# Two of twelve probability tiles turned by TensorE instead of by a transposing transfer

## The chip, the cores and the metric

The kernel runs on one core of one Trainium2 chip. Its engines work side by side, each through its own instruction stream in order: TensorE (PE in the profile, with PEld for the loading of weights), VectorE (DVE), ScalarE (ACT), GpSimd (POOL) and SyncE (SP), which here only issues DMA transfers. The metric is the device time of one execution in microseconds, as the median of several runs.

## The reference

Four images of 12288 queries with 128 channels attend to keys that are pooled out of a 384 x 32 map. Then the 128 best rows of each image go through a small MLP.

```python
kv_pool = kv.reshape(B, H//4, 4, W//4, 4, C).mean(axis=(2, 4))   # 4 x 4 pooling, 768 keys
k = v = kv_pool.reshape(B, -1, C) @ w_sr
s = (q @ k.transpose(0, 2, 1)) / sqrt(C)
a = exp(s - s.max(-1)); a /= a.sum(-1) + 1e-9
x = a @ v                                                        # (4, 12288, 128)
scores = x @ w_gate                                              # top 128 rows of each image
out[rows] = x[rows] + sigmoid(scores[rows]) * (relu(x[rows] @ w1) @ w2)
```

## The kernel before

**Blocks.** The queries are cut into 192 blocks of 256 (48 to each of four batches). A block has two halves of 128 queries (`QT = 2`), each against all 768 keys (`M = 768`, six key tiles of 128, `KT = 6`). So a block holds a 128 x 1536 score tile in PSUM: half 0 in columns 0 to 767, half 1 in 768 to 1535. Two such score buffers, `s_buf[0]` and `s_buf[1]`, alternate from block to block; each fills three PSUM banks of 512 columns.

**What happens to a block.** `S` computes its scores in four parts of three matmuls (high and low parts of q and k), in the order 3, 2, 1, 0: part 3 is columns 1024 to 1535, part 2 is 768 to 1023, part 1 is 512 to 767, part 0 is 0 to 511. `s_max` on DVE finds the row maxima of both halves. `exp` on ACT exponentiates in three pieces: part 1 is columns 768 to 1279, part 2 is columns 1280 to 1535 (the last two key tiles of half 1, `CUT = 1280`), and part 0 is columns 0 to 767. Parts 0 and 1 go to an SBUF tile `am`; part 2 is written back into the score bank. Each value is then split into an f16 high part (`to_high`, ACT) and a bf16 rest (`to_low`: DVE for the last 256 columns, POOL for the other 1280), both in the SBUF tile `hl`. `turn` (L371) transposes the high half and then the low half of `hl` into the tile `at` by one DMA transpose each, of twelve 128 x 128 tiles, issued on SP. `AV` multiplies the twelve tiles of each half by the values, in 18 matmuls for each half of the queries (36 in all), into the banks `o_two`. `sums`, `recip` and `finish` on DVE normalise the result, and each second block issues its output on SP.

**Order.** The main loop (L601 to L645) writes the order of every engine by hand: `InOrder` (L39) chains the instructions of TensorE, DVE, ACT and POOL in program order. Iteration i runs `s_max(i)`, `AV(i - 4)` in two halves, `S(i + 1)`, `exp(i, 1)`, `exp(i, 2)`, `to_high(i, 1)`, the normalising of block i - 4, `to_low(i, 1)`, `exp(i, 0)`, `to_high(i, 0)`, `turn(i, 0)`, `to_low(i, 0)` and `turn(i, 1)`. So `AV` runs four blocks behind (`LAG = 4`). The SP queue takes its transfers in the order of the program: loads of q, loads of kv, outputs and the two transposes of each block.

**Beside the blocks.** During the first three batches `next_keys` prepares the keys of the next batch, a step at a time at the marked points of the loop: kv loads of half a megabyte, pooling sums on POOL, projections on TensorE. In the last batch there is none of this. `topk` of a finished batch runs in small steps in the next one; its counts and projections borrow the score buffer of block i - 1.

**Names in the profile.** All engine instructions go through the helper at L51, so they are told by their tiles: `m<-s` is `s_max`; `am<-s,m` with 512 columns is `exp` part 1, with 768 columns part 0; `s<-s,m` is `exp` part 2; `hl<-s` is `to_high` of the last 256 columns and `hl<-am` that of the other 1280; `hl<-s,hl` is `to_low` on DVE and `hl<-am,hl` that on POOL; `at<-hl` is a DMA transpose; `o_two<-vx,at` is `AV`; `s<-kh,qh`, `s<-kl,qh` and `s<-kh,ql` are `S`.

Of the kernel before, what the change touches and what calls it, by code (L numbers as in the profile page):

```python
# [6 lines left out]
F32 = mybir.dt.float32  # L7
F32R = mybir.dt.float32r
F16 = mybir.dt.float16
BF16 = mybir.dt.bfloat16  # L10
# [3 lines left out]
AF = mybir.ActivationFunctionType  # L14
ALU = mybir.AluOpType
AX = mybir.AxisListType
HALF = 256
PSUM = bass.MemoryType.PSUM

P = 128  # L20
B, N, C = 4, 12288, 128
HK, WK, R = 384, 32, 4
M = (HK // R) * (WK // R)
# [11 lines left out]
CUT = 2 * M - HALF  # L35
# [29 lines left out]
def attention_topk_mlp(ctx, tc, a, outs, capacity):  # L65
    nc = tc.nc
    pe, dve, act, pool = (InOrder(tc, e) for e in (nc.tensor, nc.vector, nc.scalar, nc.gpsimd))
# [6 lines left out]
    qp = ctx.enter_context(tc.tile_pool(name="qp", bufs=2))  # L74
    qs = ctx.enter_context(tc.tile_pool(name="qs", bufs=3))
    wk = ctx.enter_context(tc.tile_pool(name="wk", bufs=3))
    hlp = ctx.enter_context(tc.tile_pool(name="hlp", bufs=4))
    at = ctx.enter_context(tc.tile_pool(name="at", bufs=5))
    ob = ctx.enter_context(tc.tile_pool(name="ob", bufs=3))
# [10 lines left out]
    ident, tri, jrow, wg = (cst[:, i * P:(i + 1) * P] for i in range(4))  # L90
# [7 lines left out]
    s_flat = [x.rearrange("p k q -> p (k q)") for x in s_buf]  # L98
# [3 lines left out]
    banks = [o_two[:, j] for j in range(QT)]  # L102
# [11 lines left out]
    def borrow(bank):  # L114
        room["prep"], room["select"], room["count"] = bank[:, 0:HALF], bank[:, 512:1024], bank[:, 1024:1025]
# [13 lines left out]
    def load_q(b, ch, lo=0, hi=CHUNK):  # L129
        if (b, ch) not in qraw:  # L130
            qraw[b, ch] = qp.tile([P, CHUNK], F32, name="q_raw")
        nc.sync.dma_start(out=qraw[b, ch][:, lo:hi], in_=a["q"][:, b, ch, lo:hi])
# [123 lines left out]
    def next_keys(b):  # L256
        new_keys(b)
        raws = {}
        pend = []
        ready = None  # L260

        def after(kc):
            if kc % 2:
                pair = kc // 2
                pend.extend([lambda: (split_k(b, 2 * pair, 2 * pair + 2, 0), split_k(b, 2 * pair, 2 * pair + 2, 1)),
                             lambda: v_max(b, pair)])

        for kc in range(KT):
            if kc == 0:
                raws[0] = load_kv(b, 0)  # L270
            if kc + 1 < KT:
                raws[kc + 1] = load_kv(b, kc + 1, -2)
            t = raws[kc]
            pooled = kvs.tile([P, P], F32, name="pooled")
            u = kvs.tile([P, P, TAPS // 2], F32, name="kv_sum")
            t = t.rearrange("p h k t -> p (h k) t")
            adds = [(u[:, 32 * h:32 * h + 32], t[:, 32 * h:32 * h + 32, 0:8], t[:, 32 * h:32 * h + 32, 8:16]) for h in range(4)]
            adds += [(u[:, :, 0:4], u[:, :, 0:4], u[:, :, 4:8]), (u[:, :, 0:2], u[:, :, 0:2], u[:, :, 2:4]),
                     (pooled, u[:, :, 0], u[:, :, 1])]
            for h, (o, x, y) in enumerate(adds):  # L280
                if ready and h == 1:
                    yield from key_tile(b, kc - 1, ready)
                    after(kc - 1)
                yield "d"
                pool.tensor_tensor(out=o, in0=x, in1=y, op=ALU.add)
                if h == 3 and kc + 1 < KT:
                    load_kv(b, kc + 1, -2, raws[kc + 1])
                if pend:
                    pend.pop(0)()
            ready = pooled  # L290
        yield "d"
        yield from key_tile(b, KT - 1, ready)
        after(KT - 1)
        while pend:
            yield "d"
            pend.pop(0)()
        v_peak(b)
        start(vals, v_split(b))
# [12 lines left out]
    st = {}  # L311
# [12 lines left out]
    blocks = [(b, blk) for b in range(B) for blk in range(NBLK)]  # L324

    def S(n, parts=(0, 1, 2, 3)):
        b, blk = blocks[n]
        kh, kl = kvset[b]["kh"], kvset[b]["kl"]
        qh, ql = qsplit[b, blk]
        assert b == 0 or kvset[b].get("split") == KT  # L330
        for part in parts:
            lo, hi, j, k0 = ((0, 512, 0, 0), (512, 768, 0, 512), (768, 1024, 1, 0), (1024, 1536, 1, 256))[part]
            q = slice(j * P, (j + 1) * P)
            k = slice(k0, k0 + hi - lo)
            for i, (w, x) in enumerate(((qh, kh), (qh, kl), (ql, kh))):
                pe.matmul(s_flat[n % 2][:, lo:hi], w[:, q], x[:, k], start=(i == 0), stop=(i == 2))

    def s_max(n):
        m = sm.tile([P, QT], F32, name="m")
        dve.tensor_reduce(out=m, in_=s_flat[n % 2].rearrange("p (j k) -> p j k", j=QT), axis=AX.X, op=ALU.max, negate=True)  # L340
        st[n] = {"m": m}

    def exp(n, part):
        lo, hi, j = ((0, M, 0), (M, CUT, 1), (CUT, 2 * M, 1))[part]
        if part == 1:
            st[n]["a"] = wk.tile([P, CUT], F32, name="am")
        s = s_flat[n % 2][:, lo:hi]
        r = act.activation(s if part == 2 else st[n]["a"][:, lo:hi], s, AF.Exp, bias=st[n]["m"][:, j:j + 1])
        if part == 0:
            tc.declare_no_dep(r.ins, st[n]["low"], reason="both only read, other banks")  # L350

    def split_a(n, part):
        lo, hi = ((0, CUT), (CUT, 2 * M))[part]
        if part:
            st[n]["hl"] = hlp.tile([P, 2, QT * M], U16, name="hl")
            st[n]["at"] = at.tile([P, 2, QT * KT, P], U16, name="at")
        hl = st[n]["hl"]
        return (s_flat[n % 2][:, lo:hi] if part else st[n]["a"], hl[:, 0, lo:hi].bitcast(F16), hl[:, 1, lo:hi].bitcast(BF16))

    def to_high(n, part):  # L360
        a, ah, al = split_a(n, part)
        st[n][part] = a, ah, al
        act.copy(ah, a)

    def to_low(n, part, engine):
# [3 lines left out]
            st[n]["low"] = r.ins  # L369

    def turn(n, h):  # L371
        nc.sync.dma_start_transpose(out=st[n]["at"][:, h], in_=st[n]["hl"][:, h])

    def AV(n, j, dest=None):
        vx = kvset[blocks[n][0]]["vx"]
        assert kvset[blocks[n][0]].get("ready")
        ah, al = (st[n]["at"][:, h, j * KT:(j + 1) * KT].bitcast(t) for h, t in enumerate((F16, BF16)))
        if j == 0:
            st[n]["o"] = o_all if dest is None else dest
        o = st[n]["o"][:, j]  # L380
        mm = [(ah, h, kt) for kt in range(KT) for h in range(2)] + [(al, 0, kt) for kt in range(KT)]
        for i, (w, h, kt) in enumerate(mm):
            pe.matmul(o, w[:, kt], vx[:, h, kt], start=(i == 0), stop=(i == len(mm) - 1))
# [8 lines left out]
    def recip(n):  # L392
        dve.reciprocal(st[n]["rz"], st[n]["rz"])
# [182 lines left out]
    blocks = [(b, blk) for b in range(B) for blk in range(NBLK)]  # L576
# [7 lines left out]
    def start(tasks, gen):  # L584
        tasks.append([gen, next(gen)])
# [7 lines left out]
    def at_point(point):  # L593
        advance(vals, point)
        advance(prep, point)
        advance(select, point)

    start(vals, first_values())
    nb = len(blocks)
    LAG = 4  # L600
    for i in range(nb):  # L601
        old = i >= LAG
        b, blk = blocks[i]
        if blk % 2 == 0 and i + BPC < nb:
            nb_, nblk = blocks[i + BPC]
            load_q(nb_, nblk // BPC, nblk % BPC * BLK, (nblk % BPC + 2) * BLK)
        if blk == 0 and b + 1 < B:
            start(prep, next_keys(b + 1))
        if i:
            borrow(s_flat[(i - 1) % 2])  # L610
        s_max(i)
        if old:
            AV(i - LAG, 0)
            at_point("pe")
            AV(i - LAG, 1)
        else:
            at_point("pe")
            warm(18 if i == 0 else 36, banks[0][:, 0:P])
        if i % 2 == 0 and i + 2 < nb:
            split_q(*blocks[i + 2])  # L620
        at_point("ev")
        at_point("up")
        at_point("t")
        at_point("cmp")
        at_point("g")
        if 0 < i < nb - 1:
            S(i + 1, (3, 2, 1, 0))
        exp(i, 1)
        exp(i, 2)
        to_high(i, 1)  # L630
        if old:
            sums(i - LAG)
            recip(i - LAG)
            finish(i - LAG)
        to_low(i, 1, dve)
        exp(i, 0)
        to_high(i, 0)
        turn(i, 0)
        to_low(i, 0, pool)
        turn(i, 1)  # L640
        at_point("d")
        if i in (1, 2):
            advance(vals, "d")
        if old and blocks[i - LAG][1] == NBLK - 1:
            start(select, topk(blocks[i - LAG][0]))  # L645
    ended.append(True)
    room["select"], room["count"] = banks[1], banks[0][:, 0:1]
    n = nb - 1
# [23 lines left out]
    high, low, eqh, rest = (tk.tile([P, NCOL], U16, name=x) for x in ("high", "low", "eqh", "rest16"))  # L672
# [12 lines left out]
    for m in (n - 1, n):  # L685
        norm(m)
        lo = blocks[m][1] * QT
# [78 lines left out]
```

## Time and profile before

| what | us |
|---|---|
| median of 3 runs | 1013.18 |
| lowest and highest run | 1012.69 and 1016.16 |
| the profiled execution's own time | 1014.15 |
| its span, first to last instruction | 1012.3 |

The profiled execution ran with a mean granted TensorE clock of 0.967. In the lists of instructions, a row gives the start in us from the span's start, the duration in us, the engine, the line, the operation, output and inputs by tile, and the shapes; `xN` says that N such instructions in a row are merged; a bracket at the end gives the idle time of the engine before it and what ended it. Rows of waits give the engine that waited, what it waited for, the total in us, how often, and the longest. Rows by stretch give the stretch, its length and the busy time of each engine with the number of instructions in brackets; the last three numbers are the granted TensorE clock, the busy share of the DMA engines (over 1 where packets overlap) and GB/s.

### The profile page before, as it was taken

To read this page: it belongs to the slowest core of one execution; us is meant where nothing else is said; L and a number is where in the kernel's file an instruction comes from. 1 tells how busy PE (TensorE), PEld (TensorE's weight loads), DVE (VectorE), ACT (ScalarE), POOL (GpSimd) and SP (SyncE) were. 2 spreads that over 40 slices of the span, in tenths; PEclk is the share of its full clock that TensorE was granted. 3 is DMA by queue.
4 is the path that set the end of the run, shared out by engine and by line. 5 is a ranking of instruction groups with operands and counts; after the bars stand their busy time and mean duration, and the time that the engine had idled before them with its cause. 6 is when DMAs were issued, how large, how long until landed. Compare 5 with 4: busy or idle time off the path is not lost.

```text
span 1012.3 us, 25591 instructions
## 1 busy us (share of the span) xinstructions
PE 901.4 (89%) x9779; PEld 792.3 (78%) x9779; DVE 701.0 (69%) x1732; ACT 766.3 (76%) x1162; POOL 752.9 (74%) x573
## 2 busy tenths in 40 slices
PE   3889889898998989899899989999899999999954
PEld 2778777786887877787788878888788888888843
DVE  6557656564776777576767776787867887877675
ACT  2678768776898777687788876888888888889700
POOL 1579868777798878698679886898877777777700
PEclk9989989999999999899999999999999999999966
DMA  9799999999999999999999999999999999999920
GB/s 361 206 230 233 241 232 243 235 237 232 247 231 220 247 243 238 243 244 217 246 225 243 245 234 243 232 253 233 227 240 207 231 242 230 244 225 239 211 61 6
DMA packets 674235, 230.16 MB, mean 227 GB/s; under 512 B 606016, under 2 KB 656320, under 8 KB 673344
## 3 DMA queue, kind: packets, MB, share of 16 engines
q1 hardware_dynamic: 673856, 228.00, 110.5%
q8 instruction: 77, 1.26, 0.5%
q0 software_dynamic: 256, 0.52, 0.2%
q14 instruction: 46, 0.38, 0.1%
HBM read 52.04 MB, written 25.43 MB: 77 GB/s over the span
## 4 chain that ended last, share of the span: by engine, by line
PE 40%; DMA 19%; ACT 15%; DVE 12%; issue 7%; POOL 6%; SPq 0%; POOLq 0%; DVEq 0%; ACTq 0%
PE s L51 22%; PE o_two L51 18%; DMA at<-hl 17%; DVE m L51 7%; ACT am L51 7%; ACT hl L51 5%; POOL hl L51 3%; ACT s L51 2%; DMA kv_raw<-in_kv 2%; POOL ql L51 1%; POOL kv_sum L51 1%; DVE junk L51 1%; ACT qh L51 1%; DVE hl L51 1%; ACT kv_proj L51 0%
## 5 line engine op out<-in xcount | busy, mean ns | idle before, releaser
L51 POOL TENSOR_TENSOR hl<-am,hl 128x1280 bf16<-128x1280 f32 x192 | 505.6, 2633 | 168.2 <-ACT hl L51 88.2
L51 PEld LDWEIGHTS <-at 128*128 128x128 f16 (+1 forms) x6912 | 404.6, 98 | 120.0 <-DMA at<-hl 68.5
L51 PE MATMUL o_two<-vx,at 128*128 128x130 f16 x6804 | 444.8, 221 | 54.0 <-DMA at<-hl 47.8
L51 ACT ACTIVATE am<-s,m 128x512 f32<-128x512 f32 (+1 forms) x384 | 306.7, 799 | 124.9 <-DVE m L51 76.4
L51 DVE TENSOR_REDUCE m<-s 128x2 f32<-128x1536 f32 x192 | 337.2, 1756 | 85.2 <-PE s L51 84.7
L51 PE MATMUL s<-kh,qh 128*128 128x512 f32 (+1 forms) x768 | 278.9, 363 | 8.8 <-DVE rz L51 4.0
L51 PE MATMUL s<-kh,ql 128*128 128x512 f32 (+1 forms) x768 | 260.8, 340 | 1.6 <-POOL ql L51 1.5
L51 PE MATMUL s<-kl,qh 128*128 128x512 f32 (+1 forms) x768 | 260.6, 339 | 0.0
L51 ACT CAST hl<-am 128x1280 f16<-128x1280 f32 x192 | 241.7, 1259 | 6.1
L51 PEld LDWEIGHTS s<-kh,qh 128*128 128x128 f32 x768 | 146.6, 191 | 20.5 <-ACT s L51 5.0
L51 PEld LDWEIGHTS s<-kh,ql 128*128 128x128 f32 x768 | 145.8, 190 | 19.8 <-POOL ql L51 3.6
L51 PEld LDWEIGHTS s<-kl,qh 128*128 128x128 f32 x768 | 147.4, 192 | 9.0
L51 DVE TENSOR_TENSOR hl<-s,hl 128x256 bf16<-128x256 f32 x192 | 81.2, 423 | 76.5 <-ACT hl L51 69.2
L51 POOL TENSOR_TENSOR ql<-q_raw,qh 128x512 fp32r<-128x512 f32 x96 | 123.1, 1282 | 7.0 <-ACT qh L51 7.0
L51 ACT ACTIVATE s<-s,m 128x256 f32<-128x256 f32 x192 | 86.1, 448 | 6.3
L51 DVE TENSOR_TENSOR x<-o_two,rz 128x260 f32<-128x260 f32 x189 | 81.0, 429 | 6.4
L51 DVE TENSOR_SCALAR rz<-o_two,sg 128x2 f32<-128x2 f32 x189 | 41.0, 217 | 60.3 <-PE o_two L51 59.8
L51 ACT CAST hl<-s 128x256 f16<-128x256 f32 x192 | 71.5, 373 | 6.9 <-DMA at<-hl 0.7
L51 ACT CAST qh<-q_raw 128x512 fp32r<-128x512 f32 x96 | 58.9, 613 | 1.1 <-DMA q_raw<-in_q 1.1
L51 POOL TENSOR_TENSOR kv_sum<-kv_raw 128x256 f32<-128x256 f32 x72 | 52.6, 731 | 0.0
L51 PEld LDWEIGHTS <-ones 128*128 128x128 bf16 (+1 forms) x291 | 24.5, 109 | 17.2 <-issue 13.3
L51 DVE RECIPROCAL rz<-rz 128x2 f32<-128x2 f32 x192 | 31.9, 166 | 6.6
(157 smaller groups left out, 438.9 us busy)
## 6 DMA issues: line engine op xcount, KB each, us to landing
out<-x SPq DMA_DIRECT2D x96, 256.0 KB, 3.2
q_raw<-in_q SPq DMA_DIRECT2D x93, 256.0 KB, 3.9
kv_raw<-in_kv SPq DMA_DIRECT2D x36, 512.0 KB, 5.2
kv_raw<-in_kv SPq DMA_DIRECT2D x6, 1024.0 KB, 8.4
at<-hl SPq DMA_TRANSPOSE x384, 4.6
w<-in_w SPq DMA_DIRECT2D x2, 512.0 KB, 9.5
q_raw<-in_q SPq DMA_DIRECT2D x1, 768.0 KB, 8.2
cst<-in_cst SPq DMA_DIRECT2D x1, 320.0 KB, 9.7
```

What stands on the lines that cost most here:

```text
L51: r = f(*args, **kwargs)
```

## The change

In the blocks of the first three batches (144 of 192; `by_pe`), the last two key tiles of half 1 take another way. `exp` part 2 writes to a new SBUF tile `ae` instead of back into the score bank. TensorE transposes the two 128 x 128 f32 tiles of `ae` into the place in the score bank that they came from (`turn_pe`). `to_high` and `to_low` of these 256 columns then read the transposed values from the bank and write straight into `at`. The two DMA transposes of the block shrink from twelve tiles to ten. To make room in the order, `S(i + 1)` is cut in two: parts 3 and 2, then the transposes, then parts 1 and 0; `exp` part 0 moves ahead of `to_high(i, 1)` on ACT. The last batch keeps the old way, but for the allocation of its tiles.

```diff
+    wke = ctx.enter_context(tc.tile_pool(name="wke", bufs=2))
...
+    def by_pe(n):
+        return blocks[n][0] < B - 1
+
     def exp(n, part):
         lo, hi, j = ((0, M, 0), (M, CUT, 1), (CUT, 2 * M, 1))[part]
         if part == 1:
             st[n]["a"] = wk.tile([P, CUT], F32, name="am")
-        s = s_flat[n % 2][:, lo:hi]
-        r = act.activation(s if part == 2 else st[n]["a"][:, lo:hi], s, AF.Exp, bias=st[n]["m"][:, j:j + 1])
-        if part == 0:
-            tc.declare_no_dep(r.ins, st[n]["low"], reason="both only read, other banks")
-
-    def split_a(n, part):
-        lo, hi = ((0, CUT), (CUT, 2 * M))[part]
-        if part:
             st[n]["hl"] = hlp.tile([P, 2, QT * M], U16, name="hl")
             st[n]["at"] = at.tile([P, 2, QT * KT, P], U16, name="at")
-        hl = st[n]["hl"]
-        return (s_flat[n % 2][:, lo:hi] if part else st[n]["a"], hl[:, 0, lo:hi].bitcast(F16), hl[:, 1, lo:hi].bitcast(BF16))
+        s = s_flat[n % 2][:, lo:hi]
+        if part == 2:
+            out = s
+            if by_pe(n):
+                out = st[n]["ae"] = wke.tile([P, HALF], F32, name="ae")
+        else:
+            out = st[n]["a"][:, lo:hi]
+        r = act.activation(out, s, AF.Exp, bias=st[n]["m"][:, j:j + 1])
+        if part == 0:
+            st[n]["exp0"] = r.ins
+            if "low" in st[n]:
+                tc.declare_no_dep(r.ins, st[n]["low"], reason="both only read, other banks")
+
+    def turn_pe(n):
+        for c in range(2):
+            lo = CUT + c * P
+            r = pe.transpose(s_flat[n % 2][:, lo:lo + P], st[n]["ae"][:, c * P:(c + 1) * P], ident)
+            tc.declare_no_dep(r.ins, st[n]["exp0"], reason="other banks")
+
+    def halves(n, part):
+        lo, hi = ((0, CUT), (CUT, 2 * M))[part]
+        a = s_flat[n % 2][:, lo:hi] if part else st[n]["a"]
+        if part and by_pe(n):
+            hl = [st[n]["at"][:, h, CUT // P:].rearrange("p t q -> p (t q)") for h in range(2)]
+        else:
+            hl = [st[n]["hl"][:, h, lo:hi] for h in range(2)]
+        return a, hl[0].bitcast(F16), hl[1].bitcast(BF16)
...
     def turn(n, h):
-        nc.sync.dma_start_transpose(out=st[n]["at"][:, h], in_=st[n]["hl"][:, h])
+        k = CUT if by_pe(n) else 2 * M
+        nc.sync.dma_start_transpose(out=st[n]["at"][:, h, 0:k // P], in_=st[n]["hl"][:, h, 0:k])
...
-        if 0 < i < nb - 1:
-            S(i + 1, (3, 2, 1, 0))
+        more = 0 < i < nb - 1
+        if more:
+            S(i + 1, (3, 2))
         exp(i, 1)
         exp(i, 2)
+        if by_pe(i):
+            exp(i, 0)
+            turn_pe(i)
+        if more:
+            S(i + 1, (1, 0))
         to_high(i, 1)
         if old:
             sums(i - LAG)
             recip(i - LAG)
             finish(i - LAG)
         to_low(i, 1, dve)
-        exp(i, 0)
+        if not by_pe(i):
+            exp(i, 0)
         to_high(i, 0)
         turn(i, 0)
```

More of the change, by code (lines that the diff above doesn't have):

```diff
@@ L346, in exp @@
             st[n]["a"] = wk.tile([P, CUT], F32, name="am")
-        s = s_flat[n % 2][:, lo:hi]
-        r = act.activation(s if part == 2 else st[n]["a"][:, lo:hi], s, AF.Exp, bias=st[n]["m"][:, j:j + 1])
-        if part == 0:
-            tc.declare_no_dep(r.ins, st[n]["low"], reason="both only read, other banks")
-    def split_a(n, part):
-        lo, hi = ((0, CUT), (CUT, 2 * M))[part]
-        if part:
             st[n]["hl"] = hlp.tile([P, 2, QT * M], U16, name="hl")
             st[n]["at"] = at.tile([P, 2, QT * KT, P], U16, name="at")
-        hl = st[n]["hl"]
-        return (s_flat[n % 2][:, lo:hi] if part else st[n]["a"], hl[:, 0, lo:hi].bitcast(F16), hl[:, 1, lo:hi].bitcast(BF16))
+        s = s_flat[n % 2][:, lo:hi]
[23 more added lines that the diff above has]
+        return a, hl[0].bitcast(F16), hl[1].bitcast(BF16)
     def to_high(n, part):
-        a, ah, al = split_a(n, part)
-        st[n][part] = a, ah, al
+        st[n][part] = a, ah, al = halves(n, part)
         act.copy(ah, a)
```

## The prediction

> **What bounds the kernel now.** I read the page first, then the stretches between batches, the waits in each, and the SP queue in order of time.
>
> ```profile
> span 1012.3 us, 25591 instructions
> ...
> PE 901.4 (89%) x9779; PEld 792.3 (78%) x9779; DVE 701.0 (69%) x1732; ACT 766.3 (76%) x1162; POOL 752.9 (74%) x573
> ...
> at<-hl SPq DMA_TRANSPOSE x384, 4.6
> ```
>
> PE is busiest, but no engine is full. So I split the loop at the row maxima of blocks 1, 48, 96, 144 and 191. The rows show the work on tile hl; POOL does one subtraction to a block, so its count is the number of blocks.
>
> ```profile
> 35.00:273.20 238.20, 19.83 (x47) 76.21 (x94) 123.74 (x47) 0.96 1.17 234
> 273.20:512.50 239.30, 20.32 (x49) 78.32 (x96) 126.21 (x48) 0.99 1.17 236
> 512.50:743.00 230.50, 20.28 (x48) 78.34 (x97) 126.38 (x48) 0.99 1.19 237
> 743.00:953.00 210.00, 19.94 (x47) 76.63 (x94) 124.05 (x47) 1.00 1.17 231
> ```
>
> The first three batches take 708.0 us for 143 blocks, 4.95 us each; the last takes 4.47. The DMA share and the GB/s are the same in all four, though the pace is not: a sign that transfers set it. The chain of waits shows what a block costs PE where nothing is late:
>
> ```profile
> 425.13 1.05 PE o_two L51 x18
> 426.18 0.00 PE s L51
> 426.18 1.05 PE o_two L51 x18
> 427.23 2.18 PE s L51 x12
> 429.41 1.05 PE o_two L51 x18
> ```
>
> From 425.13 to 429.41, that is 4.28 us. Over 143 blocks it makes 612 us of the 708. The waits of the four stretches, one row from each in order, say what most of the remaining 96 us are:
>
> ```profile
> PEld L51 <- DMA at<-hl: 23.8, 22, 2.7
> ...
> PEld L51 <- DMA at<-hl: 27.8, 28, 2.9
> ...
> PEld L51 <- DMA at<-hl: 10.5, 12, 2.9
> ...
> PEld L51 <- DMA at<-hl: 4.7, 6, 1.6
> ```
>
> In the three batches PE waits 62.1 us for transposed tiles, in the last 4.7. The other 34 us are projections, counts, the MLP, a lower clock in batch 0 and short waits. Why the tiles are late is seen in the SP queue, here with the POOL subtraction of one block and two rows that sum up a longer stretch (the SP transposes begun in it, and the work on hl).
>
> ```profile
> 457.57 2.62 POOL L51 TENSOR_TENSOR hl<-am,hl 128x1280 bf16<-128x1280 f32 x1 [0.89 <-ACT hl L51]
> ...
> 464.35 6.35 SPq L372 DMA_TRANSPOSE at<-hl  x2
> 470.80 0.53 SPq L408 DMA_DIRECT2D out<-x  x1
> 471.38 0.49 SPq L132 DMA_DIRECT2D q_raw<-in_q  x1
> 471.98 7.20 SPq L372 DMA_TRANSPOSE at<-hl  x4
> 479.27 0.53 SPq L408 DMA_DIRECT2D out<-x  x1
> 479.90 1.27 SPq L124 DMA_DIRECT2D kv_raw<-in_kv  x1
> 481.27 4.65 SPq L372 DMA_TRANSPOSE at<-hl  x2
> ...
> L372 SPq DMA_TRANSPOSE at<-hl x32: 1410/1802/4413, 438.6 to 517.5; - x32
> ...
> 438.50:520.70 82.20, 6.77 (x16) 26.84 (x33) 43.18 (x17) 1.00 1.18 232
> ```
>
> Each SP row begins within 0.11 us of the end of the one before: SP is never free here. The block whose subtraction ended at 460.19 has its two transposes issued only from 464.35. The stretch of 16 blocks takes 82.2 us, 5.14 a block, at 232 GB/s: this is what the SP queue and its DMA rings can do while kv is loaded, and it is slower than PE's 4.28. So in the three batches the bound alternates: transfers while the queue is backlogged, PE when it has caught up.
>
> **The change part by part.**
>
> *Smaller transposes.* A transpose moves 128 x 1536 x 2 B = 393 KB; ten tiles instead of twelve take 65.5 KB off each, 131 KB off a block. Traffic in the three batches is (238.2 x 234 + 239.3 x 236 + 230.5 x 237) / 143 = 1167 KB a block; after, 1036 KB. The last batch, without kv, moves 210.0 x 231 / 47 = 1032 KB a block. So the three batches get the traffic that batch 3 has, where PE waited 4.7 us in 47 blocks, 0.1 each. Over 143 blocks that is 14 us, and the waits fall from 62 to 14: **-48 us**. The bounds: to nothing (-62) if PE's slower pace leaves the queue still more room, and unchanged (0) if a transpose costs SP and the rings its 1.8 us whatever its size. No row has a ten-tile transpose. I take the share by size, since a plain output of 256 KB holds SP 0.53 us and a transpose 1.8: issue follows what is issued, not its number. At 232 GB/s the backlogged stretch would need (82.2 x 232 / 16 - 131) / 232 = 4.58 us a block.
>
> *Two transposes on PE.* Two f32 transposes of another tile stand between AV matmuls in the trace.
>
> ```profile
> 728.38 0.20 PEld L51 LDWEIGHTS s<-cst,mx 128*128 128x128 f32 x2
> 728.44 0.38 PE L51 MATMUL s<-cst,mx 128*128 128x128 f32 x2
> 728.65 1.13 PE L51 MATMUL o_two<-vx,at 128*128 128x130 f16 x17
> ...
> L51 PE MATMUL s<-cst,xe x3: 276/276/278, 508.6 to 953.9; 128*128 128x128 f32 x3
> ```
>
> The stream moves on after 728.65 - 728.44 = 0.21 us for both, though one shows 276 ns from its start to its modelled end. They lie fully on PE's path: 144 x 0.21 = **+30 us**, to 144 x 2 x 0.276 = 79 us if they don't overlap their neighbours. The Trainium skill (TensorE: Matmul & The Clock Gate, "Part 4: PE-mode transpose") reports about 275 ns for a bf16 transpose in one kernel, most of it access latency. Its figure is the row's duration; as an occupancy it would give the 79 us, against the 0.21 that the row's successor shows.
>
> *PE waits for ACT.* This is new: the transposes stand behind S parts 3 and 2 and wait for exp part 2; behind them queue S parts 1 and 0, and behind those the next row maxima.
>
> ```profile
> 409.79 1.76 DVE L51 TENSOR_REDUCE m<-s 128x2 f32<-128x1536 f32 x1 [0.94 <-PE s L51]
> 411.64 0.69 ACT L51 ACTIVATE am<-s,m 128x512 f32<-128x512 f32 x1 [1.90 <-DVE up L51]
> 411.66 0.50 PE L51 MATMUL s<-kh,qh 128*128 128x512 f32 x1
> 412.36 0.45 ACT L51 ACTIVATE s<-s,m 128x256 f32<-128x256 f32 x1
> 412.82 0.28 PE L51 MATMUL s<-kh,qh 128*128 128x256 f32 x1
> 412.84 0.37 ACT L51 CAST hl<-s 128x256 f16<-128x256 f32 x1
> 413.11 0.91 ACT L51 ACTIVATE am<-s,m 128x768 f32<-128x768 f32 x1
> 413.30 0.42 DVE L51 TENSOR_TENSOR hl<-s,hl 128x256 bf16<-128x256 f32 x1 [0.29 <-ACT hl L51]
> 414.05 1.26 ACT L51 CAST hl<-am 128x1280 f16<-128x1280 f32 x1
> 414.06 1.76 DVE L51 TENSOR_REDUCE m<-s 128x2 f32<-128x1536 f32 x1 [0.34 <-PE s L51]
> ```
>
> Exp part 2 ends at 412.81, and PE comes to part 1 of S (the second PE row) at 412.82. With the 0.09 us from one engine to the next (the cast ends at 413.21, DVE starts at 413.30) PE would wait 0.08 us: 12 us over 144 blocks. It is less if exp part 2, which no longer writes the bank that part 1 reads, follows it as closely as exp part 0 follows the cast (0.10 before its end) instead of 0.03 after part 1's. Between 0 and 12 I take **+6 us**. Where PE itself was late, ACT is done long before.
>
> *ACT and DVE reordered.* ACT's work is the same; only exp part 0 goes ahead of the cast, so the cast and DVE's to_low start later, and the next row maxima stand behind to_low on DVE. The loop is exp 1, exp 2, exp 0, cast, to_low, maxima: starts 0.72 and 0.48 and 0.94 apart, then 0.37 + 0.09 + 0.42 + 1.76 + 0.09 = 4.87 us if every step waits for the one before. Steps without such a wait overlap by 0.10 instead of standing 0.03 apart, 0.13 less each, so exps and cast need 0.59 + 0.35 + 0.81, and the loop 4.48: equal to PE's 4.28 + 0.21 = 4.49. I cost it at nothing, covered by PE's own block, since exp 2, exp 0 and the cast then have different outputs and no step needs the one before it on ACT. If that cover is gone, it is the rival below.
>
> *The sum:* 30 + 6 - 48 = -12 us. The profiled execution took 1014.15 us (1.9 around its span), which makes 1002; it lies 1.0 above the median of the runs, so 1001 for the median.
>
> **The rivals.**
>
> *Nothing moves (1013).* The issue of a transpose has a fixed price, or kv bursts keep the queue full. Then transfers still set the pace, and PE's 36 us fall into its 62 us of waits. For it: issue times vary from 1.4 to 4.4 us at one size. Against it: batch 3, with 1032 KB, has nearly no waits.
>
> *The DVE loop closes (1032, slower).* If ACT's steps still wait for each other, the loop of 4.87 us exceeds PE's 4.49 by 0.38. Blocks that wait for a tile anyway (22 + 28 + 12 = 62 by the rows) don't pay; the other 81 do: 31 us, 1001 + 31. For it: exp 1 and exp 2 stand 0.03 apart today, which looks like a wait. Against it: that wait goes with the in-place write. It decides as soon as the next maxima start later than PE's scores allow.
>
> *Transposes cost their duration (1050).* The 79 us instead of 30 add 49. Against it: the successor's start.
>
> *The clock falls (1020).* If two transposes in each block lower PE's activity as the clock gate counts it, the granted clock of batches 1 and 2 goes to batch 0's 0.96 too and batch 0's falls as far: 143 x 4.49 = 642 us of PE work x 0.03 = 19 us, 1020. Against it: the 0.99 to 1.00 of batches 1 to 3, where PE pauses for tiles far longer than 0.2 us. The Trainium skill (TensorE: Matmul & The Clock Gate, "Part 4: PE-mode transpose") says that a transpose doesn't count as a busy PE; the few in this trace can't show it.
>
> *All waits vanish (983).* -62 + 30 + 0 = -32, less 1 to the median gives 981 to 983.
>
> **How the numbers follow.** The forecast has 0.48 (own range 990 to 1010), nothing moves 0.19, the DVE loop 0.14, all waits vanish 0.09, transposes at duration 0.05, clock 0.05. About 0.5% (5 us) is what a measurement of this kernel can tell from no change. Of the forecast 0.06 lies within it. Faster: 0.42 + 0.09 = 0.51, and a part of the "nothing moves" case, 0.03, makes 0.54. Same: 0.06 + 0.16 = 0.22. Slower: 0.24. The range, 983 to 1030, leaves out most of the loop case and all of the transposes at duration.
>
> **What would show it.** Right: the three batches take some 696 us, PE's wait for at<-hl falls below 20 us in them, the SP rows show gaps, and a quiet stretch steps at 4.49. Transposes at about 0.1 us each by their successors' starts. Wrong: SP rows still without gaps and median issue still 1.8 us (nothing moves); maxima that wait for DVE's to_low or ACT, and quiet steps near 4.87 (the loop); PE idle before the transposes for more than 0.1 us a block.

## The result and the profile after

The changed kernel took 989.06 us (median; 987.28 to 989.85) against 1014.67 for the kernel before: a ratio of 0.974, with a 95% interval of 0.971 to 0.977. In a later comparison the same code took 989.97 us, ratio 0.981 (0.977 to 0.985). So it is faster by some 2 to 2.6%, the two intervals spanning 1.5 to 2.9%; 1001 was forecast, with a range of 983 to 1030. The profiled execution took 988.30 us, 25.9 less than the one before.

The stretches between the row maxima of blocks 1, 48, 96, 144 and 191, as before (work on tile hl; the last three numbers are clock, DMA share and GB/s):

```profile
35.00:258.50 223.50, 0.00 (x0) 59.66 (x47) 123.64 (x47) 0.98 1.12 226
258.50:489.30 230.80, 0.00 (x0) 61.71 (x49) 126.26 (x48) 0.99 1.11 220
489.30:718.80 229.50, 0.00 (x0) 61.59 (x49) 126.25 (x48) 1.00 1.04 208
718.80:925.60 206.80, 19.96 (x47) 75.95 (x94) 124.09 (x47) 1.00 1.16 229
```

The three batches take 683.8 us instead of 708.0. Their traffic rate was 234 to 237 GB/s and is now below the 229 of batch 3: transfers no longer set the pace. The backlog of the SP queue went with it. In the kernel before, SP began the first transpose of a block 4.50, 4.93 and 2.37 us (the medians of the three batches) after POOL's subtraction for that block had ended; in the changed kernel it begins 0.15, 0.02 and 1.14 us before that end. The clock is no lower than before. The chain of waits over two quiet blocks:

```profile
414.68 2.39 PE s L51 x14
417.07 1.05 PE o_two L51 x18
418.12 1.05 PE o_two L51 x18
419.17 2.41 PE s L51 x14
421.58 1.05 PE o_two L51 x18
```

A step is 4.51 us from AV to AV (417.07 to 421.58) and 4.49 from S to S (414.68 to 419.17), against 4.28: take 4.50, 0.22 more, for the two transposes among the 14 PE instructions of S. The chain of work that ended last, from the page of the profile before and then after, is now PE's:

```profile
PE 40%; DMA 19%; ACT 15%; DVE 12%; issue 7%; POOL 6%; SPq 0%; POOLq 0%; DVEq 0%; ACTq 0%
...
PE 75%; DVE 10%; ACT 5%; DMA 2%; issue 1%; SPq 0%; POOLq 0%; ACTq 0%; DVEq 0%
```

Of PE's waits (the list over the three batches, and the groups of weight loads over the whole run):

```profile
PEld s L51 <- ACT ae L51: 12.8, 22, 3.5
...
L51 PEld LDWEIGHTS s<-cst,ae 128*128 128x128 f32 x288 | 31.3, 141 | 8.5 <-ACT ae L51 7.5
L51 PEld LDWEIGHTS s<-kh,qh 128*128 128x128 f32 x768 | 146.0, 190 | 18.8 <-ACT ae L51 5.3 <-DVE mg L51 3.9
```

The list over the three batches has no row any more in which PE or PEld waits for `at<-hl`; it was 62.1 us. Of the 12.8 us that are put down to ae, only the 7.5 before the transposes' own weight loads are the new wait. The 5.3 before S's first loads were there in the kernel before under another name:

```profile
L51 PEld LDWEIGHTS s<-kh,qh 128*128 128x128 f32 x768 | 146.6, 191 | 20.5 <-ACT s L51 5.0 <-DVE mg L51 3.2 <-ACT hs L51 1.4
```

Nearly half of the 7.5 us is one wait of 3.5 us, at 287.50. Ahead of it two DVE instructions of `topk` (`key`) took 1.12 and 2.60 us, where the kernel before shows 0.41 and 0.70 for them. The second, here with the POOL subtraction beside it, held up the row maxima, and with them ACT's exps:

```profile
281.89 2.63 POOL L51 TENSOR_TENSOR hl<-am,hl 128x1280 bf16<-128x1280 f32 x1
282.04 2.60 DVE L51 TENSOR_TENSOR key<-key,sc 128x96 int32<-128x96 int32 x1
...
286.39 0.69 ACT L51 ACTIVATE am<-s,m 128x512 f32<-128x512 f32 x1 [4.73 <-DVE m L51]
```

It ends 0.12 us after POOL's subtraction; in the kernel before it ran beside a POOL sum of 0.73 us and ended 0.11 us after that. So the new order put it next to a longer POOL instruction.

The transposes themselves, in the timeline, and ACT and DVE around them:

```profile
418.96 0.69 ACT L51 ACTIVATE am<-s,m 128x512 f32<-128x512 f32 x1 [1.23 <-DVE up L51]
419.55 0.47 ACT L51 ACTIVATE ae<-s,m 128x256 f32<-128x256 f32 x1
419.90 0.90 ACT L51 ACTIVATE am<-s,m 128x768 f32<-128x768 f32 x1
420.14 0.38 PE L51 MATMUL s<-cst,ae 128*128 128x128 f32 x2
420.28 0.36 PE L51 MATMUL s<-kh,qh 128*128 128x256 f32 x1
420.48 0.28 PE L51 MATMUL s<-kl,qh 128*128 128x256 f32 x1
420.60 0.28 PE L51 MATMUL s<-kh,ql 128*128 128x256 f32 x1
420.69 0.38 ACT L51 CAST at<-s 128x256 f16<-128x256 f32 x1
421.10 0.42 DVE L51 TENSOR_TENSOR at<-s,at 128x256 bf16<-128x256 f32 x1 [0.77 <-ACT at L51]
421.62 1.76 DVE L51 TENSOR_REDUCE m<-s 128x2 f32<-128x1536 f32 x1
```

S goes on 0.14 us after the first transpose starts, and its first matmul then holds PE 0.20 us, 0.08 more than the 0.12 of the next one: together 0.22. The exps stand 0.59 and 0.35 apart, as the forecast had them. The next maxima start 0.10 us after DVE's subtraction ends, so they wait for something else: by the semaphores in the trace, 113 of the 144 maxima of the three batches start within 0.04 us of the signal of S's last matmul. So PE's path sets the step, and DVE's loop has a little room.

The SP queue, batch 1 (transposes: least, median and greatest issue time in ns), before and then after:

```profile
L372 SPq DMA_TRANSPOSE at<-hl x96: 1285/1557/5115, 272.0 to 511.4; - x96
```

```profile
L393 SPq DMA_TRANSPOSE at<-hl x97: 1253/1356/5000, 257.3 to 488.0; - x97
```

The median fell to 0.87, near 10/12 = 0.83; the least time hardly moved. So what got shorter is chiefly the part of an issue above its least time. How much of that part is a wait for the queue and how much a wait for `hl` these rows don't tell.

### The profile page after: what moved, and what is told of

Its sections match the earlier page's. It is cut to its first block, busy times and chain, and to the rows that moved or that the text cites. A ratio compares the mean times of both kernels' runs of the same rounds, so it can differ in the third digit from the quotient of the medians.

```text
span 986.5 us, 26037 instructions
## 1 busy us (share of the span) xinstructions
PE 920.9 (93%) x10067; PEld 819.4 (83%) x10067; DVE 697.9 (71%) x1732; ACT 727.1 (74%) x1162; POOL 753.4 (76%) x573
## 3 DMA queue, kind: packets, MB, share of 16 engines
q8 instruction: 79, 1.29, 0.5%
## 4 chain that ended last, share of the span: by engine, by line
PE 75%; DVE 10%; ACT 5%; DMA 2%; issue 1%; SPq 0%; POOLq 0%; ACTq 0%; DVEq 0%
PE s L51 42%; PE o_two L51 33%; DVE m L51 5%; ACT am L51 3%; DMA at<-hl 2%; DVE junk L51 2%; ACT ae L51 1%; DVE at L51 0%; DVE key L51 0%; ACT hl L51 0%; ACT at L51 0%; ACT s L51 0%; ACT kv_proj L51 0%; DVE hit L51 0%; SPq L393 0%
## 5 line engine op out<-in xcount | busy, mean ns | idle before, releaser
L51 PEld LDWEIGHTS <-at 128*128 128x128 f16 (+1 forms) x6912 | 399.8, 97 | 62.7 <-issue 55.6
L51 PE MATMUL o_two<-vx,at 128*128 128x130 f16 x6804 | 433.2, 220 | 5.4 <-POOL vx L51 2.4
L51 PE MATMUL s<-kh,qh 128*128 128x512 f32 (+1 forms) x768 | 291.1, 379 | 7.5 <-DVE rz L51 4.1
L51 ACT CAST hl<-am 128x1280 f16<-128x1280 f32 x192 | 245.2, 1277 | 1.5
L51 DVE TENSOR_TENSOR at<-s,at 128x256 bf16<-128x256 f32 x144 | 61.1, 424 | 141.8 <-ACT at L51 135.6
L51 ACT CAST at<-s 128x256 f16<-128x256 f32 x144 | 54.6, 379 | 19.0 <-PE s L51 18.8
L51 ACT ACTIVATE ae<-s,m 128x256 f32<-128x256 f32 x144 | 67.4, 468 | 0.0
L51 PE MATMUL s<-cst,ae 128*128 128x128 f32 x288 | 57.5, 281 | 4.8 <-ACT ae L51 4.6
```

Of the source, the lines that this page charges most:

```text
L51: r = f(*args, **kwargs)
```

## The experiments

Theory A: the queue of transfers was the bound of the three batches, the smaller transposes relieve it, and TensorE pays 0.22 us a block. Rival B: the gain is ACT's shorter chain, since the exps now overlap and `hl` is ready earlier. Rival C: a transfer costs the same whatever its size. A last question was whether the loop over DVE, forecast as a rival, exists at all. In the expectations, the "13 us of waits for ae" is the 12.8 of the list; the split of it into 7.5 and 5.3 was made after.

### The relief undone

Twelve tiles go by transfer again; the tiles that TensorE turned stay in the tail of `hl` and are read there.

```diff
-        k = CUT if by_pe(n) else 2 * M
+        k = 2 * M
...
+        if by_pe(n) and j == 1:
+            for h in range(2):
+                t16[h][KT - 2:] = [st[n]["hl"][:, h, CUT + c * P:CUT + (c + 1) * P] for c in range(2)]
```

> The changed kernel, but its transposing transfers keep all twelve tiles; the two tiles that TensorE turned are kept in the last 256 columns of hl and read from there by AV, and the transferred copies of these two are read by nobody. Only the relief of the transfers is undone. Theory A (the gain is the smaller transfers; TensorE's transposes cost 0.22 us a block): PE waits for at<-hl come back, over 40 us in the three batches, and the time is 1010 to 1040. Rival B (the gain is ACT's shorter chain: the exps overlap and hl is ready earlier): it stays within 10 us of 989. Rival C (each transfer costs the same whatever its size): it stays at 989 too.

Measured: 1026.68 us, ratio to the kernel before 1.013 (1.008 to 1.018). PE's waits over the three batches, which take 721.2 us:

```profile
PEld L51 <- DMA at<-hl: 28.7, 28, 3.0
```

ACT's chain is as short here as in the changed kernel, and DVE reads the bank as there. Nothing is gained: B falls as the main cause, and so does C, since the size makes 37 us between this run and the change (besides the size, only the place of the two tiles, `hl` instead of `at`, differs; the list has no wait for that). It is even 13 us slower than the kernel before: the transposes (31.5) and their waits for ae (13.0, of which 6.0 and 3.5 are two waits behind `key`) cost more than the 33 us of waits for tiles that are gone. The waits that came back are 28.7 us, not the 40 expected. PE's slower quiet step of 4.50 gives a tile more time, and so does ACT's shorter chain, by which POOL's subtraction ends 0.4 us sooner after the maxima (median 7.88 us after they start, 8.29 before). The runs don't tell the two apart.

### The relief alone

The kernel before, with ten-tile transposes and nothing else. The last two tiles of half 1 go to `at` without being turned.

```diff
+        if part and blocks[n][0] < B - 1:
+            to = [st[n]["at"][:, h, CUT // P:].rearrange("p t q -> p (t q)") for h in range(2)]
+            return s_flat[n % 2][:, lo:hi], to[0].bitcast(F16), to[1].bitcast(BF16)
...
+        k = CUT if blocks[n][0] < B - 1 else 2 * M
+        nc.sync.dma_start_transpose(out=st[n]["at"][:, h, 0:k // P], in_=st[n]["hl"][:, h, 0:k])
```

> The kernel before with ten-tile transfers in the first three batches and nothing else: exp part 2 still writes back into the bank, cast and subtraction read it there in the old order and write the last two tiles of half 1 straight into at, not turned (that part of the computation is left out). Theory A: the relief by itself, without PE's transposes and without a subtraction that reads SBUF: quiet steps 4.28 us, PE waits for at<-hl in the three batches below 20 us: 955 to 970. If DVE's subtraction from SBUF (703 ns on average against 424 from the bank) was not what made the kernel without transposes slow, this one is slow too: 1000 to 1010.

Measured: 974.43 us, ratio 0.963 (0.959 to 0.966); time and wait are both a little above what was expected. The chain over a quiet block, and the wait over the three batches (667.5 us):

```profile
426.47 1.05 PE o_two L51 x18
427.52 1.05 PE o_two L51 x18
428.57 2.15 PE s L51 x12
430.72 1.05 PE o_two L51 x18
```

```profile
PEld L51 <- DMA at<-hl: 25.0, 33, 1.9
```

The step is 4.25 us, PE's own. Size alone takes the wait from 62.1 to 25.0 us, 37 of the 62. The full change is some 15 us slower than this (16 over the three batches): that is the net price of turning two tiles on TensorE, with the new order that this needs.

### Without the transposes

The changed kernel without `turn_pe`; cast and subtraction read `ae` in SBUF.

```diff
             exp(i, 0)
-            turn_pe(i)
...
-        a = s_flat[n % 2][:, lo:hi] if part else st[n]["a"]
+        a = (st[n]["ae"] if by_pe(n) else s_flat[n % 2][:, lo:hi]) if part else st[n]["a"]
```

> The changed kernel without TensorE's two transposes: the cast and the subtraction read ae, not turned, so that the last two tiles of half 1 hold values that weren't transposed (this part of the computation is left out). Measures what the transposes and PE's wait for them cost. Theory A: 144 x 0.22 = 31 us of PE and some 13 us of waits for ae go, and the pace of the first three batches comes to that of batch 3, 4.40 us a block: 940 to 955. If the transposes were hidden behind other waits: within 10 us of 989.

Measured: 1009.24 us, ratio 0.996 (0.994 to 0.999): work left out, and 20 us slower than the change. The expectation missed. Where the time went: the subtraction of the last 256 columns, by groups, here and in the changed kernel.

```profile
L51 DVE TENSOR_TENSOR at<-ae,at 128x256 bf16<-128x256 f32 x144 | 101.2, 703 | 150.2 <-ACT at L51 145.1 <-DMA at<-hl 3.7 <-DMA out<-x 1.4
...
L51 DVE TENSOR_TENSOR at<-ae,at x144: 415/469/4722, 32.9 to 738.8; 128x256 bf16<-128x256 f32 x144
```

```profile
L51 DVE TENSOR_TENSOR at<-s,at 128x256 bf16<-128x256 f32 x144 | 61.1, 424 | 141.8 <-ACT at L51 135.6 <-DMA at<-hl 3.5 <-DMA kv_raw<-in_kv 1.7
```

With both inputs in SBUF it takes 0.70 us on average instead of 0.42; the least, median and greatest in ns (second row) show that it is a tail of long ones. In the timeline (DVE, with the POOL instruction of the same time):

```profile
417.07 1.57 DVE L51 TENSOR_TENSOR at<-ae,at 128x256 bf16<-128x256 f32 x1 [0.74 <-ACT at L51]
417.08 1.28 POOL L51 TENSOR_TENSOR ql<-q_raw,qh 128x512 fp32r<-128x512 f32 x1
...
422.90 0.43 DVE L51 TENSOR_TENSOR at<-ae,at 128x256 bf16<-128x256 f32 x1 [0.80 <-ACT at L51]
```

The first ends 0.28 us after POOL's subtraction that started with it, the second, with POOL idle, takes 0.43. All 62 of these subtractions that took over 0.60 us end 0.27 to 0.29 us after a POOL instruction. The Trainium skill (SBUF — State Buffer, "SBUF: two separate sides") says that DVE and GpSimd share a pair of ports as an exclusive lock, which a DVE instruction with two SBUF inputs contends for; the trace agrees. The late subtraction holds up the next row maxima, and the loop over DVE closes: 126 of the 142 maxima follow straight on the DVE instruction ahead of them, and S now waits for `up`, the DVE step of `topk` behind the maxima that reads a score bank, which has no row over the three batches of the changed kernel:

```profile
PEld s L51 <- DVE up L51: 21.8, 29, 4.7
```

It is the rival of the prediction, entered by another door. So this run doesn't measure the price of the transposes; the run above does.

### ACT's part alone

The same with twelve-tile transposes: cast and subtraction read `ae` and write `hl`.

```diff
-        if part and by_pe(n):
+        if False:
...
-        k = CUT if by_pe(n) else 2 * M
+        k = 2 * M
```

> Of the change only ACT's part: in the first three batches exp part 2 writes to ae instead of back into the bank, and exp part 0 comes before the cast; no transposes on TensorE, the transfers keep twelve tiles, and cast and subtraction read ae and write hl. ACT's chain from the row maxima to the last cast is some 0.4 us shorter, as in the changed kernel. Theory A: the queue still sets the pace: 1005 to 1017. Rival B (ACT's chain brings the gain): below 1000.

Measured: 1028.16 us, ratio 1.016 (1.011 to 1.021), slower than either theory said, for the reason just shown. Against the run before it, which differs only in the size of the transfers and in where the two tiles are written, it is 19 us slower. It says nothing on B by itself.

### The order alone

The kernel before, with exp part 0 ahead of the cast.

```diff
         exp(i, 1)
         exp(i, 2)
+        if blocks[i][0] < B - 1:
+            exp(i, 0)
```

> The kernel before with one change of order in the first three batches: exp part 0 goes ahead of the cast of the last 256 columns on ACT. Exp part 2 still writes back into the bank and the transfers keep twelve tiles. Tests whether the loop over DVE closes: if the steps on ACT wait for each other, the loop is up to 4.87 us, quiet steps stand at 4.6 to 4.9, and the time is 1018 to 1045. If the cast hides behind PE's work, quiet steps stay at 4.28 and the time at 1010 to 1017.

Measured: 1021.74 us, ratio 1.010 (1.007 to 1.014). ACT's timeline, with DVE's subtraction and maxima (first and second block):

```profile
402.34 0.69 ACT L51 ACTIVATE am<-s,m 128x512 f32<-128x512 f32 x1 [0.95 <-DVE up L51]
403.06 0.45 ACT L51 ACTIVATE s<-s,m 128x256 f32<-128x256 f32 x1
403.54 0.90 ACT L51 ACTIVATE am<-s,m 128x768 f32<-128x768 f32 x1
...
404.80 0.42 DVE L51 TENSOR_TENSOR hl<-s,hl 128x256 bf16<-128x256 f32 x1 [1.08 <-ACT hl L51]
405.14 1.75 DVE L51 TENSOR_REDUCE m<-s 128x2 f32<-128x1536 f32 x1
406.98 0.69 ACT L51 ACTIVATE am<-s,m 128x512 f32<-128x512 f32 x1 [1.11 <-DVE up L51]
...
411.62 0.69 ACT L51 ACTIVATE am<-s,m 128x512 f32<-128x512 f32 x1 [0.60 <-DVE up L51]
```

The loop stands at 4.64 us twice in a row, above PE's 4.28, and the maxima follow straight on the subtraction, 0.08 us before the end of its row: the loop sets the pace of the quiet blocks. With exp part 2 written in place the exps stand 0.72 and 0.48 apart, in the change 0.59 and 0.35. These 0.26 us are what keeps the loop of the changed kernel (4.64 - 0.26 = 4.38 by these numbers) under PE's 4.50. Its own timeline gives about the same room: there the maxima start 0.10 us after the subtraction instead of 0.08 before its end, and 4.51 - 0.18 = 4.33.

### The change in all batches

```diff
-        return blocks[n][0] < B - 1
+        return True
```

> The change in the last batch too, where PE waits only 2 to 5 us for transferred tiles. Theory A: 48 x 0.22 = 11 us of PE more, at most 5 us of waits less: 994 to 1001. Rival (any smaller transfer pays, whatever waits there are): 980 to 986.

Measured: 1001.02 us, ratio 0.990 (0.984 to 0.995). The last batch takes 222.4 us instead of 206.8 with the same three batches ahead (683.9). Its row, with the work on tile m:

```profile
718.50:940.90 222.40, 82.56 (x47) 86.82 (x141) 0.99 0.96 188
```

47 x 0.22 = 10 us for the transposes; their waits for ae rose from 7.5 to 13.9 us, 4.3 of it in one wait behind `key`. Where the queue has little to relieve, the price stands alone.

### Fewer blocks

In every second block, and in two of three.

```diff
-        return blocks[n][0] < B - 1
+        return blocks[n][0] < B - 1 and n % 2 == 0
```

```diff
-        return blocks[n][0] < B - 1
+        return blocks[n][0] < B - 1 and n % 3 != 2
```

> The changed kernel with TensorE's transposes in every second block of the first three batches only. Theory A: half of PE's cost (16 us) and of its waits for ae (6 us) go, half of the relief of the transfers too; with 1102 KB a block instead of 1036 some 15 to 25 us of waits for at<-hl come back: 980 to 995. If the relief matters only as a whole: above 1000.

> The changed kernel with TensorE's transposes in two of three blocks of the first three batches. Theory A: 10 us of PE and 4 us of waits for ae go, 5 to 12 us of waits for at<-hl come back: 980 to 990, about as the change. If every block's relief counts: 1000 or more.

Measured: 1004.21 us, ratio 0.991 (0.988 to 0.995), and 1001.62, ratio 0.991 (0.988 to 0.994). Both are slower than the change, and both expectations were too low. The waits over the three batches, every second block first:

```profile
PEld L51 <- DMA at<-hl: 28.4, 33, 2.2
```

```profile
PEld L51 <- DMA at<-hl: 15.6, 18, 3.6
```

With two thirds of the relief 15.6 us of waits come back for 10.5 us of PE and 4.5 of waits for ae saved. The 11 us that this kernel is slower in the three batches lie almost all in its other waits (the rest in the table below), and no run shows why.

### A later place for the transposes

```diff
-            S(i + 1, (3, 2))
+            S(i + 1, (3, 2, 1))
...
-            S(i + 1, (1, 0))
+            S(i + 1, (0,))
```

> The changed kernel with part 1 of S ahead of TensorE's transposes too (parts 3, 2, 1, then the transposes, then part 0). PE comes to the transposes 0.35 us later, so its waits for ae fall from 13 us to below 6; the cast, to_low and the next row maxima start some 0.2 us later. If the DVE loop still has that room: 980 to 987. If the maxima now wait for to_low so that the loop over DVE sets quiet steps (over 4.55 us): 992 to 1010.

> The changed kernel as it is, beside the variant on the same chip: 985 to 994, PE waits for at<-hl under 5 us in the first three batches.

Measured: 993.03 us, ratio 0.983 (0.980 to 0.987), against 989.97 and 0.981 (0.977 to 0.985) for the change beside it: not told apart. The transposes' waits for ae went from 7.4 to 6.1 us only. PE's later arrival is no cure, since these waits aren't 0.08 us in each block, but a few longer ones, up to 3.5 us. It also uses up the room of the loop over DVE: 142 of the 144 maxima now follow straight on DVE's work, and quiet steps are 4.53 us, just short of the 4.55 that the expectation named for this case.

## Why the prediction was right

The three batches split into the same terms in each run in which the loop over DVE doesn't set the pace (us). PE's own work is 143 x 4.28; the transposes are 0.22 for each block that has them; the waits are PEld's for `at<-hl` and the transposes' for ae; the rest is the remainder.

| kernel | three batches | PE's own | transposes | wait at<-hl | wait ae | rest |
|---|---|---|---|---|---|---|
| before | 708.0 | 612 | 0 | 62.1 | 0 | 34 |
| relief alone | 667.5 | 612 | 0 | 25.0 | 0 | 31 |
| the change | 683.8 | 612 | 31.5 | 0 | 7.5 | 33 |
| relief undone | 721.2 | 612 | 31.5 | 28.7 | 13.0 | 36 |
| two of three blocks | 694.5 | 612 | 21.0 | 15.6 | 3.0 | 43 |
| every second block | 695.7 | 612 | 15.8 | 28.4 | 3.6 | 36 |

- **The bound.** Right: transfers in the SP queue, shown by the relief undone (no gain), the relief alone (the largest gain) and the backlog. One sign for it was weak. The prediction read SP rows without gaps as an SP that is never free; in the changed kernel the rows from 409.23 to 439.71 also start within 0.11 us of the end of the one before, though PE waits for no transfer there. What does tell the two kernels apart is the delay between a block's subtraction and its transposes. (The backlogged block at 232 GB/s comes to 4.57 us by the prediction's own numbers, not 4.58.)
- **Two transposes on PE, +30.** Right: 31.5, 0.22 a block against 0.21. The 276 ns from start to end, the rival at 1050, is not what they occupy.
- **PE waits for ACT, +6.** Right in size, 7.5, by luck; wrong in kind. In a quiet block PE doesn't wait, and 3.5 of the 7.5 are the one wait behind `key`.
- **Smaller transposes, -48.** This is the mis-sized step: -62, the lower bound given for it, which named PE's slower pace as its reason; the sum left that out. The forecast carried over batch 3's wait of 0.1 us a block because the traffic is the same. At PE's old pace that was too good: the relief alone leaves 25.0 us, not 14, and is worth -37. With the transposes and the new order these 25.0 us go as well. The two terms were priced apart, and they aren't independent: what TensorE pays is partly given back by waits that are no longer met. The price of the transposes is 39 us by its parts, but only 683.8 - 667.5 = 16 in time. That the slower step alone does this is argued, not shown: ACT's shorter chain came with it. The order alone, with twelve tiles, the slow step (4.64) and not the overlapping exps, brings the wait from 62.1 to 44.7 only.
- **ACT and DVE reordered, nothing.** Right, and nearer than it looked: the order alone costs 9 us, and only the removal of the in-place write makes the room, 0.12 to 0.18 us. The closed loop measured 4.64, not 4.87.
- **The sum.** -12 was forecast, -25.9 came. The smaller transposes, 14 us beyond their term, make the 13.9 us between the two; the other differences, of 1 to 3 us, cancel to nothing. Batch 3 became 3.2 us shorter with unchanged work, and its length in the kernels that leave it alone spans 206.8 to 211.4, so that this is not taken as an effect.
- **The rivals.** "Nothing moves" is refuted by the relief alone, the clock by its column (0.98, 0.99, 1.00 against 0.96, 0.99, 0.99), and the loop over DVE is real but stays under PE's step. "All waits vanish", at 983, came nearest and had only 0.09; the time lies 1 us outside the forecast's own 990 to 1010. The stated range held it because this rival was taken in.

Left open: what is behind the other 4 us of the waits for ae, none over 0.7 us, and whether `key` would be short again at another place in the order. No run changed either.

## What to carry to other kernels

When two resources take turns as the bound, work moved from the one to the other can be worth more than the sum of the terms priced one by one, as here, where waits that the relief alone left were gone at the slower step: price the relief at the new pace and the new order. A wait total on the relieved resource gives the largest gain, and the quiet step of the engine that takes the work gives the cost; here that was 62 us against 31. A queue without gaps isn't yet a queue that is late: look at how long it starts after its data is ready. Before work is left out to measure it, see where the operands then lie: a subtraction that moved from PSUM to SBUF cost more than the transposes that were left out.

## What was not expected of the hardware

- A DVE subtraction of 128 x 256 took 0.42 us with one operand in PSUM and 0.70 us on average with both in SBUF, 4.7 at most; each that took over 0.60 us ended 0.27 to 0.29 us after a POOL instruction.
- The second of two small DVE instructions of `topk` (128 x 96) took 2.60 us beside a POOL subtraction of 2.63 us and 0.70 us beside a POOL sum of 0.73, and ended 0.11 to 0.12 us after each.
- Two ACT instructions in a row stood 0.03 us apart where the second wrote in place the bank that both read, and overlapped by 0.10 us where it wrote elsewhere: 0.72 against 0.59 us from start to start.
- The least issue time of a transposing transfer was 1.29 us for twelve tiles and 1.25 for ten (batch 1), 2.5% less; the median in a busy queue fell by 13%.
